# Gate and value of the last two blocks in seven half products, over named PSUM banks, with the last quarters in another order

## The chip, the core and the metric

The kernel runs on one core of a Trainium2 chip. The core has a matrix engine (TensorE, in the profile PE for matmuls and PEld for the loads of their stationary operand), VectorE (DVE), ScalarE (ACT), GpSimd (POOL) and SyncE (SP, which here only issues DMAs). They run side by side, each through its own instructions in order, and wait for each other by semaphores. SBUF is the working memory. PSUM is eight banks of 128 partitions by 512 fp32, into which TensorE writes; VectorE and ScalarE read and write PSUM too.

The metric is the time of one execution on the device in microseconds. The kernel before takes 343.21 us, the median of 7 runs between 342.92 and 343.62.

## What is computed

An attention without softmax and a gated feed-forward layer behind it:

```python
kv  = einsum('bhsd,bhse->bhde', k, v)            # 8 batches, 8 heads, 576 tokens, 64 wide
o   = einsum('bhsd,bhde->bhse', q, kv)
x   = o / sqrt(mean(o * o, -1) + 1e-6) * g_norm  # then 4608 tokens x 512
ffn = (gelu(x @ w_gate) * (x @ w_val)) @ w_out   # 512 -> 1536 -> 512
out = x + sigmoid(x @ w_res) * ffn
```

`x @ w_gate` and `x @ w_val` are called gate and value here, and `gelu(gate) * value` is the hidden tensor `hid`.

## The kernel before

**Blocks.** The 4608 tokens are worked in nine blocks of 512. Blocks 0 to 7 are the first 512 tokens of the eight batches; block 8 holds the remaining 64 tokens of every batch. The main loop (at the end of the kernel, `for blk in range(B + 1)`) writes the order of the work out by hand: a block is a list of `slots`, and after slot `s` come the pieces that `plans[blk][s]` holds. The engines keep the order in which the pieces are written.

**Slots of a block.** Slots 0 to 11 are `m_gval(blk, f)`, one for each of twelve strips `f` of 128 hidden columns: four matmuls of 128x512 for the gate, four for the value, a Gelu on ScalarE (L324) and a product on VectorE (L325) into `hid`. Slots 12 and 13 are `m_res` (L356), four times four matmuls for the residual gate, each followed by a Tanh on ScalarE (L365). Slots 14 and 15 are the product with `w_out`. In block 0 that is a plain product (`out_by_f`). In blocks 1 to 7 (`out_by_products`) it is one step of the scheme of Strassen and Winograd: both operands are cut into 2x2 quarters, and seven products of quarters (12 matmuls of 128x256 each, L431), with sums of quarters before and after them, take the place of eight. The sums of the `hid` quarters are `s_begin` (after slot 8) and `s_rest` (after slot 11), three chained VectorE operations of 128x1536 (L404); those of `w_out` were made in blocks 0 and 1. The products run on TensorE in the order A, D, A, E, A, F, A: `wA` holds running sums, `wE` starts as a copy of `wA` by ScalarE (L456), `wd` is a copy of `wD` (L458), `wF` is the sum of `wA` and `wd` by VectorE (L404). A finished quarter is multiplied with the sigmoid by VectorE (`pf`, L466) and gets `x` added by GpSimd (`fin`, L470), and SyncE stores it. Between `pf((0, 0))` and the sum `c22` stands a hook, `rest`, for pieces of other work; only block 1 uses it.

**Attention beside it.** The attention of batch b runs in the slots of block b - 1: raw loads on the GpSimd queue (`load_behind`), kv product, o product, squares and sums (L222, L224), the norm (`a_norm`, many small VectorE operations after slot 7), `a_t` (L282) and `a_x` (L296) after slots 9 to 11, and a DMA transpose into `xT` on the SyncE queue (L313, after slot 12). For b = 2, 3, 5 and 7 the remaining tokens of two batches get their `a_t` and `a_x` after slot 15 of block b - 1. So blocks 7 and 8 have no attention beside them.

**The last block.** `out_last` is the same seven products for block 8, with `wA` split in two halves, a fourth `m_res` in the middle of the products, and stores from two queues (SyncE and ScalarE, L533).

**The opening.** Batch 0 is worked by a list of words, `opening`, that interleaves loads, casts, transposes, the attention of head pairs 0 to 3 and the first eight matmul groups. `o1` and `o0` (L734) write two PSUM tiles of the pool `pmoe`; `t0` (L759, VectorE) is the last reader of the tile of `o0`; the words `g1` and `v1` (L785) start two gate tiles and two value tiles, of strips 0 and 1, for head pair 1.

**PSUM.** Two pools of four banks, `pmoe` for the feed-forward layer and `pattn` for attention. A tile that is asked for gets a bank of its pool that has come free, in the order of the program as written. The first writer of a tile waits until every reader of the former tile in its bank is done.

Of the kernel before, what the change touches and what calls it, by code (L numbers as in the profile page):

```python
# [8 lines left out]
FP32 = mybir.dt.float32  # L9
FP16 = mybir.dt.float16  # L10
# [8 lines left out]
def kernel(  # L19
# [33 lines left out]
    attnp = ctx.enter_context(tc.tile_pool(name="attnp", bufs=2))  # L53
    xp = ctx.enter_context(tc.tile_pool(name="xp", bufs=3))
    hidp = ctx.enter_context(tc.tile_pool(name="hidp", bufs=1))
    moep = ctx.enter_context(tc.tile_pool(name="moep", bufs=3))
    finp = ctx.enter_context(tc.tile_pool(name="finp", bufs=2))

    pmoe = ctx.enter_context(tc.tile_pool(name="pmoe", bufs=4, space=bass.MemoryType.PSUM))
    pattn = ctx.enter_context(tc.tile_pool(name="pattn", bufs=4, space=bass.MemoryType.PSUM))  # L60

    ctx.enter_context(tc.manual_schedule())
    nc.scalar.preload_act_table_set("sqrt_and_others")
# [78 lines left out]
    def new_block(blk):  # L142
        pool, kw = (xp, {}) if blk < B else (consts, {})
        t_t[blk] = pool.tile([P, NJ, C], FP16, tag="t" if blk < B else "tl", name="t")
        xT_t[blk] = pool.tile([P, NJ, NP, P], FP16, tag="xT" if blk < B else "xTl", name="xT")

    def attn_begin(b):
        st[b] = {
# [201 lines left out]
        m_mm(vps, wv_c, f, blk, 0, NJ)  # L350
        m_act(blk, f, gps, vps)

    def m_res(blk, j, pool=pmoe, tag="mm"):
        rps = pool.tile([P, C], FP32, tag=tag, name="rps")
        for cc in range(NP):
            nc.tensor.matmul(  # L356
                rps,
                lhsT=xT_t[blk][:, j, cc, :],
                rhs=wr16[:, cc, :],
                start=(cc == 0),  # L360
                stop=(cc == NP - 1),
            )

        th = th_all[:, j, :]
        nc.scalar.activation(out=th, in_=rps, func=AF.Tanh, scale=0.5)  # L365
        return th
# [70 lines left out]
                    skip_group_check=True,  # L437
                )

    def out_by_products(blk, later, rest=()):  # L440
        w = {}
        s_ = hid_sums

        def res(jj):
            for j in (2 * jj, 2 * jj + 1):
                m_res(blk, j)
            if jj == 1:

                pmoe.tile([P, C], FP32, tag="mm", name="none")

        def first_two():
            for n in ("D", "E", "F", "A"):
                w[n] = pmoe.tile([P, 2, CH], FP32, tag="mm", name="w" + n)
            w["d"] = finp.tile([P, 2, CH], FP32, tag="wd", bufs=1, name="wd")
            prod(w["A"], a_of(blk, 1, 1), b_of(1, 1), True)
            nc.scalar.copy(out=w["E"], in_=w["A"])  # L456
            prod(w["D"], s_[0], wo_t[:, 0], True)
            nc.scalar.copy(out=w["d"], in_=w["D"])  # L458
            for j in range(NJ):
                m_sigmoid(j)  # L460
# [48 lines left out]
            at(blk + 1, 10, lambda: fin((1, 1)), lambda: store(1))  # L509
        return [lambda: res(0), lambda: res(1), first_two, others]  # L510

    def out_last(blk):

        s_ = hid_sums

        def bank(n, pool, tag):
            return pool.tile([P, n, CH], FP32, tag=tag, name="w")

        def part(j, n, ch):
            return slice(None), slice(j, j + n), slice(ch * CH, (ch + 1) * CH)  # L520

        def gated(j, n, ch, src):
            of = part(j, n, ch)
            nc.vector.tensor_tensor(out=res_all[of], in0=th_all[of], in1=src, op=ALU.mult)  # L524

        def plus(j, n, ch, eng):
            of = part(j, n, ch)
            eng.tensor_tensor(out=res_all[of], in0=res_all[of], in1=t_t[blk][of], op=ALU.add)  # L528

        def store(j, n, c0, c1):  # L530
            for e, queue in enumerate((nc.sync, nc.scalar)):
                dst = out.rearrange("(j e s) c -> e s j c", e=2, s=S)[e, M0:S, j : j + n, c0:c1]
                queue.dma_start(out=dst, in_=res_all[e * R : (e + 1) * R, j : j + n, c0:c1])  # L533

        def run():
            wa = [bank(1, pattn, "at") for _ in range(2)]
            wd, we, wf = [bank(2, pmoe, "mm") for _ in range(3)]
            d = finp.tile([P, 2, CH], FP32, tag="wd", bufs=1, name="wd")
            for e in range(2):
                prod(wa[e], a_of(blk, 1, 1), b_of(1, 1), True, (e,))  # L540
                nc.scalar.copy(out=we[:, e : e + 1, :], in_=wa[e])
            prod(wd, s_[0], wo_t[:, 0], True)
            nc.scalar.copy(out=d, in_=wd)
            for j in range(NJ - 1):
                m_sigmoid(j)
            for e in range(2):
                prod(wa[e], s_[1], wo_t[:, 1], False, (e,))
                sub(nc.vector, wf[:, e : e + 1, :], wa[e], d[:, e : e + 1, :], ALU.add)
            prod(we, a_of(blk, 1, 2), b_of(2, 1), False)
            gated(0, 2, 0, we)  # L550
            plus(0, 2, 0, nc.gpsimd)
            m_res(blk, 3)
            m_sigmoid(3)
            prod(wf, s_[3], b_of(2, 2), False)
            gated(0, 2, 1, wf)
            plus(0, 2, 1, nc.gpsimd)
            store(0, 2, 0, C)
            for e in range(2):
                prod(wa[e], s_[2], wo_t[:, 2], False, (e,))
                sub(nc.vector, res_all[part(2 + e, 1, 1)], wa[e], d[:, e : e + 1, :], ALU.add)  # L560
            gated(2, 2, 1, res_all[part(2, 2, 1)])
            plus(2, 2, 1, nc.gpsimd)
            store(2, 2, CH, C)
            for e in range(2):
                prod(wa[e], a_of(blk, 2, 2), wo_t[:, 3], False, (e,))
                gated(2 + e, 1, 0, wa[e])
            plus(2, 1, 0, nc.gpsimd)
            plus(3, 1, 0, nc.vector)
            store(2, 2, 0, CH)

        return [lambda: [m_res(blk, j) for j in range(3)], run]

    def out_by_f(blk):

        ths, fpss, pfs = [], [], []
        slots = [lambda j=j: ths.append(m_res(blk, j)) for j in range(NJ)]

        def step(f):
            if f == 0:
                fpss.extend(pmoe.tile([P, C], FP32, tag="mm", name="fps") for _ in range(NJ))  # L580
            for j in range(NJ):
                m_ffn(blk, j, f, fpss[j])
            if NFH <= f < NFH + NJ:
# [153 lines left out]


    def f_sq(pr, j0, j1):
        first["sq", pr, j0] = sq = attnp.tile([P, j1 - j0, 2, D], FP32, tag=f"sq{j1 - j0}", name="sq")  # L740
        ps = first["o", pr].rearrange("p j (h d) -> p j h d", h=2)
        nc.scalar.activation(out=sq, in_=ps[:, j0:j1], func=AF.Square)

# [155 lines left out]
    def plan_attn(b):  # L899
# [36 lines left out]
        if rem:  # L936
            at(m, NF + 3, lambda: a_x(b, NJ), lambda: d_xT(b, NJ, NJ + 1))

    late = []
    for blk in range(B + 1):  # L940
        plan = plans[blk]
# [8 lines left out]
            plan[5] = [lambda j=j: a_x(0, j) for j in range(NJ)]  # L950
        else:
            slots = [lambda f=f: m_gval(blk, f) for f in range(NF)]
            if blk == 1:
                slots[0] = lambda: m_gval(1, 0, pattn, "at")
                plan.setdefault(3, []).append(lambda: (wo_sums(1), wo_sums(3)))
            outs = []
            slots += [lambda i=i: outs[i]() for i in range(4 if blk < B else 2)]
            plan.setdefault(NFH + 2, []).insert(0, lambda: s_begin(blk))
            def products(blk=blk, outs=outs):
                s_rest(blk)  # L960
                outs.extend(out_by_products(blk, blk == 1, amid_out.get(blk, ())) if blk < B else out_last(blk))

            plan.setdefault(NF - 1, []).append(products)
            for j, fs in enumerate(late):
# [55 lines left out]
```

## Time and profile before

| what | value |
|---|---|
| median of 7 runs | 343.21 us (342.92 to 343.62) |
| the execution that was profiled | 343.19 us |
| its span, first to last instruction | 341.4 us |
| granted clock of TensorE, mean | 0.996 |
| busy: TensorE matmuls / weight loads | 331.0 us (97%) / 186.8 us |
| busy: VectorE, ScalarE, GpSimd | 231.5, 150.1, 102.3 us |
| block 7: first gate matmul, first `m_res`, first matmul of block 8 | 267.81, 288.53, 301.15 us |
| block 8: first `m_res`, first product, last product's start | 321.87, 324.46, 333.27 us |

Times of single instructions are counted from the start of the span. 1.79 us of the profiled execution lie outside its span. A matmul's row gives its issue and a modelled end, so matmuls in a row overlap in the records; the distance of their starts is what one costs.

### The profile page before, as it was taken

The page shows a single profiled execution, that of the slowest core. Times are in us where ns is not written, and L with a number is a line of the kernel's source. Part 1 is how long each engine was busy: PE and PEld are TensorE (multiplying, and loading weights), DVE is VectorE, ACT ScalarE, POOL GpSimd, SP SyncE. Part 2 cuts the span into 40 slices and gives each one's busy share as a digit, 9 for nine tenths or more (in the row PEclk, how much of TensorE's full clock was granted, in tenths as well). Part 3 has the DMA queues.
Part 4 walks back from the last instruction along what each step waited for, and adds up shares of the span by engine and source line. Part 5 has one row for each costly group of instructions (what it writes and reads, how often), then busy time and mean ns, then how long its engine had stood idle before and what let it go on. Part 6 is the DMA issues. An engine that isn't in the chain of part 4 may idle for free.

```text
span 341.4 us, 6156 instructions
## 1 busy us (share of the span) xinstructions
PE 331.0 (97%) x2432; PEld 186.8 (55%) x2432; DVE 231.5 (68%) x439; ACT 150.1 (44%) x265; POOL 102.3 (30%) x121
## 2 busy tenths in 40 slices
PE   8899999999999999999999999999999999999992
PEld 3544454446744485448444854485447644854481
DVE  6755369489859976797479776975787745453643
ACT  3663464364354433544354525352636233523450
POOL 2782334960055029001900182004000600050013
PEclk9999999999999999999999999999999999999998
DMA  8999999599699156916591539563003210030004
GB/s 243 317 201 200 195 203 168 138 155 94 140 145 170 40 118 154 187 9 139 144 181 10 123 127 175 47 126 139 2 0 61 83 57 2 1 122 3 0 2 123
DMA packets 76399, 38.81 MB, mean 114 GB/s; under 512 B 42066, under 2 KB 73810, under 8 KB 76370
## 3 DMA queue, kind: packets, MB, share of 16 engines
q0 software_dynamic: 38752, 17.17, 40.2%
q1 hardware_dynamic: 37184, 20.71, 21.9%
q10 hardware_dynamic: 434, 0.52, 0.5%
q8 instruction: 19, 0.31, 0.4%
q14 instruction: 10, 0.08, 0.1%
HBM read 38.80 MB, written 9.44 MB: 141 GB/s over the span
## 4 chain that ended last, share of the span: by engine, by line
PE 90%; DVE 4%; DMA 3%; issue 1%; POOL 1%; POOLq 0%; SPq 0%; DVEq 0%
PE gps L336 27%; PE vps L336 26%; PE wA L431 10%; PE rps L356 8%; PE fps L373 3%; PE wD L431 3%; PE wF L431 3%; PE wE L431 3%; PE w L431 2%; PE kvp L187 2%; DMA hid_s<-in_v_dram 1%; DMA kf<-in_k_dram 1%; PE op L205 1%; DVE t L282 1%; DVE t L759 1%
## 5 line engine op out<-in xcount | busy, mean ns | idle before, releaser
L324 ACT ACTIVATE ge<-gps 128x512 f16<-128x512 f32 x108 | 64.3, 597 | 131.9 <-PE gps L336 126.6
L325 DVE TENSOR_TENSOR hid<-ge,vps 128x512 f16<-128x512 f16 x108 | 73.7, 684 | 63.6 <-PE vps L336 59.4
L336 PE MATMUL vps<-xT,wv 128*128 128x512 f16 x424 | 108.8, 379 | 0.4 <-DVE hid L325 0.4
L336 PE MATMUL gps<-xT,wg 128*128 128x512 f16 x424 | 109.0, 379 | 0.0
L470 POOL TENSOR_TENSOR osb<-osb,t 128x512 f32<-128x512 f32 x28 | 36.1, 1310 | 154.4 <-DVE osb L466 148.6
L336 PEld LDWEIGHTS <-wv 128*128 128x128 f16 x424 | 41.5, 98 | 50.6 <-issue 0.7
L336 PEld LDWEIGHTS <-wg 128*128 128x128 f16 x424 | 40.2, 98 | 45.4 <-issue 0.4
L431 PEld LDWEIGHTS <-hid_s 128*128 128x128 f16 x384 | 37.5, 98 | 5.1 <-DVE hid_s L404 0.4
L356 PE MATMUL rps<-wr,xT 128*128 128x512 f16 x144 | 32.7, 379 | 0.0
L431 PEld LDWEIGHTS <-hid 128*128 128x128 f16 x288 | 28.2, 98 | 5.1
L365 ACT ACTIVATE th<-rps 128x512 f32<-128x512 f32 x36 | 21.5, 598 | 19.0 <-PE rps L356 19.0
L356 PEld LDWEIGHTS <-xT 128*128 128x128 f16 x144 | 14.1, 98 | 16.8
L224 DVE TENSOR_REDUCE ss<-sq 128x8 f32<-128x512 f32 x32 | 20.6, 679 | 2.9 <-ACT sq L222 2.7
L431 PE MATMUL wA<-wo_ts,hid_s 128*128 128x256 f16 x168 | 20.6, 273 | 0.0
L370 ACT ACTIVATE th<-th 128x512 f32<-128x512 f32 x36 | 19.9, 622 | 0.0
L282 DVE TENSOR_TENSOR t<-op,ny 128x512 f16<-128x512 f32 x28 | 17.8, 680 | 0.1
L222 ACT ACTIVATE sq<-op 128x512 f32<-128x512 f32 x28 | 15.3, 596 | 4.5 <-PE op L205 4.1
L296 DVE TENSOR_TENSOR t<-t,g 128x512 f16<-128x512 f16 x36 | 16.2, 496 | 0.1
L404 DVE TENSOR_TENSOR hid_s<-hid 128x1536 f16<-128x1536 f16 x16 | 15.3, 954 | 0.3
L528 POOL TENSOR_TENSOR osb<-osb,t 128x512 f32<-128x512 f32 (+1 forms) x4 | 4.3, 1079 | 27.8 <-DVE osb L524 27.8
L373 PE MATMUL fps<-wo,hid 128*128 128x512 f16 x48 | 11.2, 379 | 0.0
L431 PE MATMUL wD<-wo_ts,hid_s 128*128 128x256 f16 x84 | 10.3, 273 | 0.1
(132 smaller groups left out, 316.5 us busy)
## 6 DMA issues: line engine op xcount, KB each, us to landing
out_dram<-osb SPq DMA_DIRECT2D x14, 512.0 KB, 2.7
qraw<-in_q_dram POOLq DMA_DIRECT2D x7, 512.0 KB, 8.0
k<-in_k_dram POOLq DMA_DIRECT2D x7, 512.0 KB, 9.7
v<-in_v_dram POOLq DMA_DIRECT2D x7, 512.0 KB, 11.9
out_dram<-osb SPq DMA_DIRECT2D x5, 256.0 KB, 2.8
wg<-in_moe_w_gate_dram POOLq DMA_DIRECT2D x2, 512.0 KB, 8.2
wv<-in_moe_w_val_dram POOLq DMA_DIRECT2D x2, 512.0 KB, 8.9
wo<-in_moe_w_out_dram POOLq DMA_DIRECT2D x2, 512.0 KB, 13.7
```

What stands on the lines that cost most here:

```text
L224: nc.vector.tensor_reduce(out=out_, in_=sq, op=ALU.add, axis=mybir.AxisListType.X)
L282: nc.vector.tensor_tensor(out=t, in0=o, in1=scale, op=ALU.mult)
L296: nc.vector.tensor_tensor(out=t_t[blk][:, jj, :], in0=t_t[blk][:, jj, :], in1=g16, op=ALU.mult)
L324: nc.scalar.activation(out=ge, in_=gps, func=AF.Gelu)
L325: nc.vector.tensor_tensor(out=hids[blk][:, f, :], in0=ge, in1=vps, op=ALU.mult)
L336: nc.tensor.matmul(ps[:, j0 * P : j1 * P], lhsT=w[:, cc, :], rhs=xT_t[blk][:, j0:j1, cc, :], start=(cc == 0 and j0 == 0), stop=(cc == NP - ...
L356: nc.tensor.matmul(rps, lhsT=xT_t[blk][:, j, cc, :], rhs=wr16[:, cc, :], start=(cc == 0), stop=(cc == NP - 1),)
L365: nc.scalar.activation(out=th, in_=rps, func=AF.Tanh, scale=0.5)
L370: nc.scalar.activation(out=th, in_=th, func=AF.Copy, scale=0.5, bias=0.5)
L373: nc.tensor.matmul(fps, lhsT=hids[blk][:, f, j * P : (j + 1) * P], rhs=wo16[:, f, :], start=(f == 0), stop=(f == NF - 1))
L431: nc.tensor.matmul(ps[:, e - es[0], :], lhsT=a[:, f, e * P : (e + 1) * P], rhs=b[:, f, :], start=(start and e == es[0] and f == 0), stop=( ...
L470: nc.gpsimd.tensor_tensor(out=res_all[of], in0=res_all[of], in1=t_t[blk][of], op=ALU.add)
```

## The change

**Named banks.** A class `Banks` takes the place of the two pools' choice: a tile gets the next bank of a fixed turn, or the bank that its caller names. `pmoe` owns banks 0 to 3 (the first three tiles 0, 1, 2, then the turn 3, 2, 1, 0 over and over), `pattn` banks 4 to 7. `banks_behind()` names the banks of the residual tiles and of A, D, E, F behind twelve strips; A gets the bank of the last strip's value tile.

**Seven half products.** In blocks 7 and 8 the slots 0 to 11 become three calls of `gv_group`, each for four strips (512 hidden columns). Gate and value of a group are each the product of x (512 tokens by 512) with a 512x512 piece of weights, cut into 2x2 quarters: seven products of four matmuls of 128x256 (the word `1g` is product 1 of the gate) for what eight would be. ScalarE copies A into E and the D product out of F (`E`, `d`), VectorE makes F and the fourth quarter c from A and d (`F`, `c`), ScalarE takes the Gelu of each quarter (`g11` and so on), VectorE three products into `hid` and GpSimd the fourth (`h22`, from SBUF alone). Gate and value have four banks each.

**Sums for it.** Weight sums (24 of 128x512 in fp16; the eight of group 0 as two instructions of 128x256 each) are made by VectorE after slots 0, 1, 2, 5 and 6 of blocks 3 to 6, into four new tiles and two buffers of `q16`. Token sums (four of 128x512 for each of blocks 7 and 8) are made by VectorE in the hook `rest` of blocks 6 and 7.

**The last block.** All four `m_res` stand ahead of the products; the sigmoids run in the order 2, 3, 0, 1; GpSimd prepares `u = th * d + t` for the quarter (rows 2 and 3, second half), which VectorE then finishes with two products and one sum of 128x512; VectorE adds x to the last quarter row by row; the first store is split in two.

**Small ones.** The pool of the Gelu outputs has 5 buffers for 3, `xT` has 2 for 3, the squares of the opening share one tag.

```diff
-    pmoe = ctx.enter_context(tc.tile_pool(name="pmoe", bufs=4, space=bass.MemoryType.PSUM))
-    pattn = ctx.enter_context(tc.tile_pool(name="pattn", bufs=4, space=bass.MemoryType.PSUM))
+    psum = ctx.enter_context(tc.tile_pool(name="psum", bufs=1, space=bass.MemoryType.PSUM))
+    class Banks:
+        def __init__(self, *turn, opening=()):
+            self.turn, self.opening = list(turn), list(opening)
+        def tile(self, shape, dtype, name, tag=None, bank=None):
+            if bank is None and self.opening:
+                bank = self.opening.pop(0)
+            elif bank is None:
+                bank = self.turn.pop(0)
+                self.turn.append(bank)
+            return psum.tile(shape, dtype, tag=f"bank{bank}", name=name)
+    pmoe, pattn = Banks(3, 2, 1, 0, opening=(0, 1, 2)), Banks(4, 5, 6, 7)
+    def banks_behind():
+        g0, v0, g1, v1 = pmoe.turn
+        pmoe.turn = [g1, v0, g0, v1]
+        return {0: g0, 1: g1, 2: v0, 3: g0, "A": v1, "D": g1, "E": v0, "F": g0}
...
         def run():
...
-            for j in range(NJ - 1):
+            for j in (2, 3, 0, 1):
                 m_sigmoid(j)
...
+            sub(nc.gpsimd, u, th_all[part(2, 2, 1)], d, ALU.mult)
+            sub(nc.gpsimd, u, u, t_t[blk][part(2, 2, 1)], ALU.add)
             prod(we, a_of(blk, 1, 2), b_of(2, 1), False)
             gated(0, 2, 0, we)
             plus(0, 2, 0, nc.gpsimd)
-            m_res(blk, 3)
-            m_sigmoid(3)
+            store(0, 2, 0, CH)
             prod(wf, s_[3], b_of(2, 2), False)
             gated(0, 2, 1, wf)
             plus(0, 2, 1, nc.gpsimd)
-            store(0, 2, 0, C)
+            store(0, 2, CH, C)
             for e in range(2):
                 prod(wa[e], s_[2], wo_t[:, 2], False, (e,))
-                sub(nc.vector, res_all[part(2 + e, 1, 1)], wa[e], d[:, e : e + 1, :], ALU.add)
-            gated(2, 2, 1, res_all[part(2, 2, 1)])
-            plus(2, 2, 1, nc.gpsimd)
+                gated(2 + e, 1, 1, wa[e])
+            of = part(2, 2, 1)
+            sub(nc.vector, res_all[of], res_all[of], u, ALU.add)
             store(2, 2, CH, C)
             for e in range(2):
                 prod(wa[e], a_of(blk, 2, 2), wo_t[:, 3], False, (e,))
                 gated(2 + e, 1, 0, wa[e])
-            plus(2, 1, 0, nc.gpsimd)
-            plus(3, 1, 0, nc.vector)
+                plus(2 + e, 1, 0, nc.vector)
             store(2, 2, 0, CH)
...
+    def token_sums(blk, eng):
...
+        return [
+            lambda: one(0, (0, 1), (0, 0)),
+            lambda: one(1, (1, 1), 0),
+            lambda: one(2, (1, 1), (0, 1)),
+            lambda: one(3, (1, 0), 1),
+        ]
+    def gv_group(blk, g, banks, amid=()):
...
+        for word in """1g 1v Eg 5g Ev 5v dg 6g dv 6v Fg 2g Fv 2v 7g g11 7v cg 3g cv 3v h11 g22 4g g12 h12 * 4v g21 h22 h21""".split():
...
+    units = [(n, g) for g in range(NF // GF) for n in "gv"]
+    all_sums = [f for u in units for f in weight_sums(u, nc.vector)]
+    sums_in = {3: all_sums[0:5], 4: all_sums[5:10], 5: all_sums[10:16], 6: all_sums[16:24]}
+    SUM_SLOTS = (0, 0, 1, 2, 2, 5, 5, 6)
...
+            sevens = blk in LAST
+            if sevens:
+                slots = [None] * NF
+                ends = banks_of(blk)
+                mid = [lambda: s_begin(blk)]
+                for g in range(NF // GF):
+                    slots[GF * g] = lambda g=g: gv_group(blk, g, ends[g], mid if g == 2 else ())
...
+            if blk + 1 in LAST:
+                amid_out.setdefault(blk, []).extend(token_sums(blk + 1, nc.vector))
```

In `one(i, x, y)` a number names an earlier sum of the same four: the second token sum reads the first, and the fourth the second. In `gv_group` the word list gives the order in which the pieces are written: a digit first is a product on TensorE, `E` and `d` are ScalarE's copies, `F` and `c` VectorE's sums, `g11` to `g22` the Gelus, `h11` to `h22` the products into `hid`, and `*` in the third group is `s_begin`.

## The prediction

> **What bounds the kernel.** I read the page's first and fourth part, then the chain of waits from 118 us on.
>
> ```profile
> PE 331.0 (97%) x2432; PEld 186.8 (55%) x2432; DVE 231.5 (68%) x439; ACT 150.1 (44%) x265; POOL 102.3 (30%) x121
> PE 90%; DVE 4%; DMA 3%; issue 1%; POOL 1%; POOLq 0%; SPq 0%; DVEq 0%
> ```
>
> TensorE is the bound: from 21 us to the last product it has one hole in the records (0.44 at 113.8), so a matmul saved there is time saved, and any wait put ahead of a matmul is time lost. The chain gives prices by issue:
>
> ```profile
> 288.69 3.45 PE rps L356 x16
> 292.15 1.31 PE wA L431 x12
> ```
>
> A 128x512 matmul costs 3.45 / 16 = 0.2158 us, a 128x256 one 1.31 / 12 = 0.1092.
>
> **What the half products take away.** A block's gate and value are 96 matmuls of 128x512, 20.72 us (block 7: 267.81 to 288.53). After, 3 x 2 x 7 x 4 = 168 of 128x256: 18.35. That is 2.37 less per block, **-4.75 us** for two, if nothing waits.
>
> **Do the groups keep pace?** A product takes 0.437. A consumer starts 0.20 after its product's last issue (block 6: twelve from 258.64 end issuing at 259.95, ScalarE starts at 260.15). Counted from a group's start: products 1g, 1v, 5g, 5v end at 0.44, 0.87, 1.31, 1.75; ScalarE's four copies (0.57 to 0.59 each, L456, L458) end at 1.23, 1.78, 2.35, 2.90; VectorE's F sums (0.70, L404; a next one can start after 0.60) run 2.40 to 3.10 and 3.00 to 3.70. 7g is due at 3.49, 7v at 3.93: 0.18 to spare. Sums c end at 4.85 and 5.45; 4v is due at 5.68: again 0.18. ScalarE is busy 4.7 and VectorE 4.8 of 6.11 us. So a steady group costs nothing, narrowly; every bank that it takes over had its last reader earlier. Below zero is excluded: TensorE can't go faster than issue.
>
> **The opening.** The turn is 3, 2, 1, 0 behind 0, 1, 2. `idle` has bank 0, `o1` 1, `o0` 2; so the gate tiles of `g1` get 3 and 2, and the second must wait for the last reader of `o0`, `t0`. Today it is the second *value* tile that gets that bank:
>
> ```profile
> 16.34 0.59 PE L785 MATMUL gps<-xT,wg 128*128 128x512 f16 x2 [0.24 <-ACT xT L776]
> 16.77 0.39 PE L769 MATMUL xtp<-ident,t 128*128 128x128 f16 x4
> 17.01 0.39 PE L785 MATMUL vps<-xT,wv 128*128 128x512 f16 x1
> 17.99 0.38 PE L785 MATMUL vps<-xT,wv 128*128 128x512 f16 x1 [0.59 <-DVE t L759]
> ```
>
> The wait for `t` is there now, but behind the transposes of pair 2. After, they stand behind it: they go from 16.77 to 18.20, and ScalarE's copy of them from 17.19 to 18.62. On ScalarE the root of pair 3 (17.78) is queued behind that copy, on VectorE the reciprocal and both halves of `t3` (18.41 to 19.17) behind the root: now until 20.6. `g0`, at 19.52 today behind the transposes of `t3`, comes at 20.77. From there both run at matmul pace: **+1.25 us**. Bounds: 0, were the bank free earlier, and 1.43, the whole shift.
>
> The hole in TensorE grows from 0.59 to 1.43. The granted clock stayed at 1.00 from 15.20 to 18.60 us, where TensorE was busy 2.56 of 3.40 us; I cost it at nothing. The Trainium skill ("TensorE: Matmul & The Clock Gate", "A second HAM failure mode: psum-queue depth-cycling") speaks against this change here: many short idles between groups of matmuls can bring the clock to half. By that page's window of 3.4 us one such fall would add an estimated 1.7 us to the sum.
>
> **Bank A.** The first product of a block's output now takes the bank of strip 11's value, so it waits for the last `hid`; today it has a residual's bank. In block 2:
>
> ```profile
> 117.98 0.68 DVE L325 TENSOR_TENSOR hid<-ge,vps 128x512 f16<-128x512 f16 x1
> 118.10 1.47 PE L431 MATMUL wA<-wo,hid 128*128 128x256 f16 x12
> 119.71 1.48 PE L431 MATMUL wD<-wo_ts,hid_s 128*128 128x256 f16 x12
> ```
>
> `wA` moves to 118.71 and `wD` to 120.02: +0.31 (strip 10's value also waits longer, which this swallows). Blocks 4 and 6 have `hid` ending within 0.01 of `wA`'s start: +0.06 each. **+0.43 us**; bounds 0 and 0.8.
>
> **Weight sums.** An fp16 sum of 128x512 has the nearest row in L296, 0.415 us. They hide in VectorE's holes ahead of the strips: in block 6 it waits 1.04, 1.04, 1.47, 1.40 us for TensorE ahead of strips 0 to 3 and 0.39, 1.04 ahead of 6 and 7, for eight sums of 3.3 us together; the last has its end at 248.1, strip 7 is ready at 248.55. **0**; bound above 0.4 per block, one sum late, 1.6.
>
> **Token sums.** These have no such hole. VectorE in the output of block 6, from the timeline:
>
> ```profile
> 264.25 0.69 DVE L466 TENSOR_TENSOR osb<-th,wE 128x512 f32<-128x512 f32 x1 [0.71 <-ACT th L370]
> 265.45 0.69 DVE L404 TENSOR_TENSOR osb<-wA,wd 128x512 f32<-128x512 f32 x1 [0.51 <-PE wA L431]
> 268.69 0.87 DVE L282 TENSOR_TENSOR t<-o,ny 128x512 f16<-128x512 f32 x1
> 269.59 1.26 DVE L296 TENSOR_TENSOR t<-t,g 128x512 f16<-128x512 f16 x1
> ```
>
> GpSimd in the same timeline, its second add there:
>
> ```profile
> 268.97 1.60 POOL L470 TENSOR_TENSOR osb<-osb,t 128x512 f32<-128x512 f32 x1
> ```
>
> The operation of L296 in the whole run (shortest, median, longest in ns):
>
> ```profile
> L296 DVE TENSOR_TENSOR t<-t,g x36: 409/415/1266, 29.0 to 269.6; 128x512 f16<-128x512 f16 x36
> ```
>
> The four sums stand between the first two lines, and the last A product (issue at 266.50) must wait until the second, `c22`, has read `wA`. Alone: sums at 264.85, 265.31 (it reads the first), 265.64, 265.98; `c22` 266.30 to 267.00; A at 267.05, +0.55. But GpSimd starts its add at 265.01, right in them, and the L296 line shows what that does: beside an add the same operation took 1.26, ending 0.28 after the add ended (270.57). The add in turn stood still while `t` (268.69) ran, took its turn between `t` and L296, which reads `t`, and lasted 1.60 for 1.16. So: first sum to 265.27, the add to 266.28, second sum to 266.56, `c22` 267.15 to 267.84, A at 267.89: +1.39. I take this, the nearest row being the same operation: **+2.78 us** for blocks 6 and 7; bounds 1.1 and 3.3 (the add goes first). The Trainium skill ("SBUF — State Buffer", "Who interferes with whom") calls such a meeting a lock that whoever issues first holds for its whole instruction. By that page the sum is +2.78 and the upper bound falls away, for the first sum issues before the add; the rows alone leave it open.
>
> **Block 7's first group.** At its start VectorE still has `pf`, `t` and L296 of the remaining tokens. Today its next operation starts at 270.78, 2.97 after the block's start; Fg is due at 2.40 and 7g at 3.49 needs it 0.70 later, so 7v waits: +0.39. With the block's end later, the adds fall ahead of `t` as well as of L296; Fg starts at 3.5, 7g at 4.25 for 3.49, 7v 0.16 later still: **+0.92**. I take the second, which goes on from the step before; bounds 0.2 and 1.3. Block 8 has only `pf` in front, done at 0.95: 0.
>
> **The tail.** Counted from the first product of block 8, the last is issued at 9.17 before and after (the fourth `m_res` only moves). Today the last sum ends 2.07 behind that (336.65 against 334.58), and the end of the span comes 4.75 later with the store. After, GpSimd has u (two of 1.15, from the sigmoid at 4.55 on), then the two adds, until 9.24; VectorE's sum with u reads two SBUF tiles at 8.5, so it waits for the second add and ends at 9.8; then product, add, product, add of 0.43 each with gaps: 11.4, that is 2.23 behind: **+0.16**. Without the meeting it is 1.68: -0.39; bounds -0.4 and +0.5. Three early stores of 0.6 us issue lie ahead of it.
>
> **Sum.** -4.75 + 1.25 + 0.43 + 0 + 2.78 + 0.92 + 0.16 = +0.79. The profiled execution took 343.19, 0.02 below the median: **344.0 us**.
>
> **Rivals.**
> *The meeting doesn't bite* (the other side, not slower): the four sums run through ahead of the add. Place: after `pf((0, 0))` of blocks 6 and 7. Tokens 1.1, first group 0.2, tail -0.39: -4.75 + 1.25 + 0.43 + 1.1 + 0.2 - 0.39 = -2.16, 341.0. For it: the first sum issues before the add. Against: three L296 at 1.26. It ends faster as soon as the two stalls are under 0.65 each with the rest as forecast. Chance 0.24.
> *The opening isn't touched*: `t0` moves ahead or the bank is free: 344.0 - 1.25 = 342.7. Against: the wait on `t` stands in the rows. 0.08.
> *The groups don't keep pace*: three steps in a chain (copy, copy, F) each 0.1 later use up the 0.18 twice per group; 0.24 x 6 = +1.5: 345.4. For it: no row has this chain. 0.16.
> *The halves cost more than 0.1092*: the moving operand comes in two runs of 128. Against: today's runs are 128 long and issue at pace. At 0.1233 the gain is gone: 348.7. 0.02.
>
> **Chances.** The forecast has 0.50, its own range 343.0 to 345.1, 0.18 of it under 343.9. What 7 runs can tell from no change is 0.2%, 0.69 us. Faster: 0.24 and a little of the second rival, 0.26. Same: 0.18 and most of the second rival, 0.25. Slower: 0.32 + 0.16 + 0.02, 0.49. The range reaches from the first rival to the third: 341.0 to 345.5.
>
> **What would show it.** Block 7's 168 matmuls of gate and value in 19.3 us and block 8's in 18.35; a TensorE wait on `t` L759 at `gps`; on `osb` L404 ahead of the last `wA` of blocks 6 and 7, 1.3 to 1.4 each, with a token sum of over 1.1 us; on F at block 7's start. No such waits and a start of block 8 more than 4 us early: the first rival. Waits on F and c in all six groups: the third.

## The result and the profile after

The changed kernel takes 343.7 us (median of 27 runs) where the kernel before takes 343.39 (64 runs): a ratio of 1.0003, 95% interval 0.9992 to 1.0014. The difference can't be told from none. Medians are over all runs, while ratios leave out the few in which a kernel took some per cent longer at a lower granted clock, so a ratio is not the quotient of two medians. The profiled execution took 344.5 us, with a span of 342.6 and a granted clock of 0.995.

The same two parts of the page as before, busy time and the chain:

```profile
PE 327.5 (96%) x2576; PEld 200.8 (59%) x2576; DVE 257.6 (75%) x498; ACT 161.2 (47%) x289; POOL 110.2 (32%) x127
PE 86%; DVE 6%; DMA 3%; ACT 2%; issue 1%; POOL 0%; SPq 0%; DVEq 0%
```

TensorE has 3.5 us less to do, and the span is not shorter. VectorE has 26 us more, and its share of the chain went from 4 to 6%. So the place to look is TensorE's waits (what waited, for whom, total us, times, longest). These four are the ones that bear on the change:

```profile
PE wA L452 <- DVE osb L425: 2.3, 2, 1.2
PE gps L957 <- DVE t L931: 1.3, 1, 1.3
PE Ag L682 <- DVE Fg L703: 0.8, 1, 0.8
PE vps L357 <- DVE hid L346: 0.8, 1, 0.8
```

The first three were not there before; `vps` on `hid` was, with 0.4, and a `vps` waited 0.6 for `t`. The list also has `idle` with 1.2, as before, and two waits of `kvp` on `v` ahead of block 0, 0.8 and 0.7 where they were 0.6 and 0.2. For each of the first three I read the timeline.

**The opening**, TensorE. The second gate tile of `g1` waits where a value tile waited before, and the transposes (L941) stand behind it:

```profile
17.21 0.38 PE L957 MATMUL gps<-xT,wg 128*128 128x512 f16 x1 [0.24 <-POOL wg L984]
18.88 0.38 PE L957 MATMUL gps<-xT,wg 128*128 128x512 f16 x1 [1.29 <-DVE t L931]
19.09 0.38 PE L941 MATMUL xtp<-ident,t 128*128 128x128 f16 x4
```

**The output of block 6**, VectorE, GpSimd and the last A product. L488 is GpSimd's addition of x, the four `ts` are the token sums:

```profile
267.55 0.42 DVE L425 TENSOR_TENSOR ts<-xT 128x512 f16<-128x512 f16 x1
267.71 1.27 POOL L488 TENSOR_TENSOR osb<-osb,t 128x512 f32<-128x512 f32 x1 [29.07 <-DVE osb L484]
268.00 1.26 DVE L425 TENSOR_TENSOR ts<-xT,ts 128x512 f16<-128x512 f16 x1
269.19 0.41 DVE L425 TENSOR_TENSOR ts<-xT 128x512 f16<-128x512 f16 x1
269.52 0.41 DVE L425 TENSOR_TENSOR ts<-xT,ts 128x512 f16<-128x512 f16 x1
269.86 0.68 DVE L425 TENSOR_TENSOR osb<-wA,wd 128x512 f32<-128x512 f32 x1
270.59 1.47 PE L452 MATMUL wA<-wo_ts,hid 128*128 128x256 f16 x12 [1.23 <-DVE osb L425]
```

The second sum needs 0.42 us and takes 1.26. It ends at 269.26, 0.28 behind the end of GpSimd's addition (268.98). `c22`, the line with `osb<-wA,wd`, stands behind all four sums and starts late by their time and by the 0.84 us that the second takes too long. The A product, which must wait until `c22` has read `wA`, waits 1.23.

**The start of block 7**, GpSimd, VectorE and the product 7g:

```profile
271.21 4.22 POOL L488 TENSOR_TENSOR osb<-osb,t 128x512 f32<-128x512 f32 x3 [2.23 <-DVE osb L484]
272.77 1.64 DVE L303 TENSOR_TENSOR t<-o,ny 128x512 f16<-128x512 f32 x1
274.44 1.27 DVE L317 TENSOR_TENSOR t<-t,g 128x512 f16<-128x512 f16 x1
275.63 0.68 DVE L703 TENSOR_TENSOR Fg<-Ag,d 128x512 f32<-128x512 f32 x1
276.37 0.60 PE L682 MATMUL Ag<-ts,ws 128*128 128x256 f16 x4 [0.82 <-DVE Fg L703]
```

The two steps of the remaining tokens take 2.9 us beside GpSimd's three additions, where they took 0.87 and 1.26 in the kernel before, and Fg comes 3.74 us after the block's start (271.89).

A table of stages puts these into one sum. A stage is the distance of two starts of issue: "gv" from a block's first gate matmul to its first `m_res`, "out" from there to the next block's first gate matmul. Tail: from the last product's end of issue to the last sum. Store: from there to the end of the span. Stages that are not named differ by 0.01 at most.

| stage (us) | before | after | difference |
|---|---|---|---|
| start of block 0 | 16.34 | 17.21 | +0.87 |
| gv 0 | 22.18 | 23.46 | +1.28 |
| out 1 | 12.81 | 12.92 | +0.11 |
| gv 2 and out 2 | 36.23 | 36.55 | +0.32 |
| gv 3 to gv 6 (weight sums) | 89.74 | 89.74 | 0 |
| out 4 | 12.62 | 12.68 | +0.06 |
| out 6 | 12.62 | 14.07 | +1.45 |
| gv 7 | 20.72 | 19.48 | -1.24 |
| out 7 | 12.62 | 13.90 | +1.28 |
| gv 8 | 20.72 | 18.34 | -2.38 |
| out 8 | 12.70 | 12.64 | -0.06 |
| tail | 2.08 | 2.21 | +0.13 |
| store | 4.75 | 4.12 | -0.63 |

Without the first line the differences add to +0.32, and the medians differ by +0.31. I don't count the first line to the change: the program up to there does the same work in all fourteen profiles of this study, and block 0 starts anywhere between 16.04 and 17.86 in the thirteen of the changed kernel and its variants, which has the 16.34 of the kernel before inside. Nor "out 1": it is 12.80 or 12.81 in all thirteen others.

So the half products give what their count says, and five new delays, less a shorter store, leave nothing of it.

### The profile page after: what moved, and what is told of

It is laid out like the page before. It is cut to its first block, busy times and chain, and to the rows that moved or that the text cites. A ratio compares the mean times of both kernels' runs of the same rounds, so it can differ in the third digit from the quotient of the medians.

```text
span 342.6 us, 6525 instructions
## 1 busy us (share of the span) xinstructions
PE 327.5 (96%) x2576; PEld 200.8 (59%) x2576; DVE 257.6 (75%) x498; ACT 161.2 (47%) x289; POOL 110.2 (32%) x127
## 4 chain that ended last, share of the span: by engine, by line
PE 86%; DVE 6%; DMA 3%; ACT 2%; issue 1%; POOL 0%; SPq 0%; DVEq 0%
PE gps L357 21%; PE vps L357 20%; PE wA L452 9%; PE rps L377 8%; PE Av L682 3%; PE Ag L682 3%; PE fps L394 3%; PE wD L452 3%; PE w L452 2%; PE wF L452 2%; PE wE L452 2%; DMA kf<-in_k_dram 2%; PE kvp L208 2%; PE Fv L682 2%; PE Fg L682 2%; DMA hid_s<-in_v_dram 2%
## 5 line engine op out<-in xcount | busy, mean ns | idle before, releaser
L345 ACT ACTIVATE ge<-gps 128x512 f16<-128x512 f32 x84 | 50.1, 597 | 98.6 <-PE gps L357 97.8
L357 PE MATMUL vps<-xT,wv 128*128 128x512 f16 x328 | 84.2, 379 | 0.8 <-DVE hid L346 0.8
L357 PE MATMUL gps<-xT,wg 128*128 128x512 f16 x328 | 84.4, 380 | 0.0
L346 DVE TENSOR_TENSOR hid<-ge,vps 128x512 f16<-128x512 f16 x84 | 57.2, 682 | 32.8 <-PE vps L357 28.9
L488 POOL TENSOR_TENSOR osb<-osb,t 128x512 f32<-128x512 f32 x28 | 36.2, 1312 | 138.9 <-DVE osb L484 133.1
L357 PEld LDWEIGHTS <-wv 128*128 128x128 f16 x328 | 32.1, 98 | 39.6 <-issue 1.1
L357 PEld LDWEIGHTS <-wg 128*128 128x128 f16 x328 | 30.7, 98 | 34.7 <-DMA xT<-t 0.2
L682 PEld LDWEIGHTS <-ws 128*128 128x128 f16 x192 | 18.8, 98 | 3.3 <-issue 1.2
L719 POOL TENSOR_TENSOR hid<-ge,c 128x512 f16<-128x512 f16 x6 | 7.0, 1166 | 25.6 <-ACT ge L713 25.6
L452 PE MATMUL wA<-wo_ts,hid 128*128 128x256 f16 x84 | 10.3, 272 | 2.3 <-DVE osb L425 2.3
```

The lines of the kernel that those rows point to most:

```text
L345: nc.scalar.activation(out=ge, in_=gps, func=AF.Gelu)
L346: nc.vector.tensor_tensor(out=hids[blk][:, f, :], in0=ge, in1=vps, op=ALU.mult)
L357: nc.tensor.matmul(ps[:, j0 * P : j1 * P], lhsT=w[:, cc, :], rhs=xT_t[blk][:, j0:j1, cc, :], start=(cc == 0 and j0 == 0), stop=(cc == NP - ...
L452: nc.tensor.matmul(ps[:, e - es[0], :], lhsT=a[:, f, e * P : (e + 1) * P], rhs=b[:, f, :], start=(start and e == es[0] and f == 0), stop=( ...
L488: nc.gpsimd.tensor_tensor(out=res_all[of], in0=res_all[of], in1=t_t[blk][of], op=ALU.add)
L682: nc.tensor.matmul(out_[:, r, :], lhsT=lhsT, rhs=rhs, start=(first and r == 0 and c == 0), stop=(c == 1), skip_group_check=True,)
```

## The experiments

My theory: each delay is a separate stage with the cause named in the prediction (bank of the opening, bank A, the meeting of VectorE and GpSimd over the token sums, the remaining tokens in front of Fg). Rivals: VectorE's work is too much wherever GpSimd stands; or what one repair frees is waited for elsewhere. Unless said, an edit is to the changed kernel alone.

### The opening's banks

```diff
-    pmoe, pattn = Banks(3, 2, 1, 0, opening=(0, 1, 2)), Banks(4, 5, 6, 7)
+    pmoe, pattn = Banks(3, 2, 1, 0, opening=(1, 2, 0)), Banks(4, 5, 6, 7)
```

> The changed kernel with the first three named banks as 1, 2, 0 in place of 0, 1, 2, so that strip 1's value tile, not its gate tile, gets the bank of o0. Theory (the opening pays for the bank order): the wait of 1.3 us of a gate tile on t goes, 0.6 of it comes back at the value tile, g0 comes 1.25 to 1.28 earlier, and the time falls by that from the changed kernel's, to about 342.3. Rival (the opening is paced by its loads and casts, the wait lies in their shadow): within 0.3 us of the changed kernel, 343.5.

Measured: 342.6 us (9 runs), ratio to the kernel before 0.9982 (0.9972 to 0.9992). The timeline of this kernel, TensorE:

```profile
16.82 0.59 PE L957 MATMUL gps<-xT,wg 128*128 128x512 f16 x2 [0.24 <-ACT xT L948]
17.25 0.39 PE L941 MATMUL xtp<-ident,t 128*128 128x128 f16 x4
18.48 0.38 PE L957 MATMUL vps<-xT,wv 128*128 128x512 f16 x1 [0.63 <-DVE t L931]
```

Both gate tiles run at once, the transposes follow, and the value tile waits 0.63 as it did before. gv 0 is 22.19 for 23.46, a gain of 1.27; the median is 1.1 lower. The theory holds.

### The token sums ahead of the quarter

```diff
             prod(w["E"], a_of(blk, 1, 2), b_of(2, 1), False)
+            ahead = blk + 1 in LAST
+            for f in rest if ahead else ():
+                f()
             pf((0, 0), w["E"])
-            for f in rest:
+            for f in () if ahead else rest:
                 f()
```

> The changed kernel with the four token sums of blocks 6 and 7 ahead of pf((0, 0)) in place of behind it, so before GpSimd's add begins and in a hole of 0.7 us. Theory (the sums meet GpSimd's add, and the last A product waits for c22): the waits of 1.23 and 1.12 us of wA on osb go, no token sum is over 0.5 us, and the time falls by 2.6 to 3.3, to about 340.7. Rival (VectorE has no room there, 1.4 us of sums cost that wherever they stand): c22 is as late as before or the A product ahead of it waits for F, and the time falls by less than 1.

Measured: 340.25 us (4 runs), ratio 0.9908 (0.9895 to 0.9921). Block 6's output in the timeline:

```profile
265.49 0.42 DVE L425 TENSOR_TENSOR ts<-xT 128x512 f16<-128x512 f16 x1
265.94 0.42 DVE L425 TENSOR_TENSOR ts<-xT,ts 128x512 f16<-128x512 f16 x1
266.28 0.42 DVE L425 TENSOR_TENSOR ts<-xT 128x512 f16<-128x512 f16 x1
266.61 0.42 DVE L425 TENSOR_TENSOR ts<-xT,ts 128x512 f16<-128x512 f16 x1
...
267.55 0.69 DVE L425 TENSOR_TENSOR osb<-wA,wd 128x512 f32<-128x512 f32 x1
267.71 1.15 POOL L488 TENSOR_TENSOR osb<-osb,t 128x512 f32<-128x512 f32 x1 [29.74 <-DVE osb L484]
268.54 1.47 PE L452 MATMUL wA<-wo_ts,hid 128*128 128x256 f16 x12
```

The sums take up the 0.71 us in which VectorE waited for the sigmoid and delay the quarter by the rest, which holds up no product: the A product has no wait, and out 6 and out 7 are 12.68 and 12.62. There is a second thing to see: `c22` (267.55) runs beside GpSimd's addition and neither is longer than alone, 0.69 and 1.15. It reads one operand from PSUM; the sums that suffered read two from SBUF. The kernel before shows the same with GpSimd first: `c22` at 265.45, 0.44 us into the addition that starts at 265.01, took 0.69 (the row and the addition's start stand in the prediction). Block 7's gate and value gained too (18.71 for 19.48), because the remaining tokens' first step now takes 0.87 us for 1.64; that is why the time fell by 3.45 us, more than the 2.6 to 3.3 that were expected.

### GpSimd's addition behind the next one

```diff
-            if not later:
-                fin((0, 0))
...
+            fin((0, 0))
```

The second line stands behind `fin((0, 1))`; the token sums stay where the change has them.

> The token sums stay where the change has them, and only GpSimd's first addition of a block's end is moved, behind the one that follows it, so that it no longer runs beside the token sums. Theory (the meeting): without GpSimd beside them the four sums take about 0.42 us each instead of 0.42, 1.26, 0.41 and 0.41, so the last A product of blocks 6 and 7 waits some 0.84 us less each: 14.07 and 13.90 us fall to about 13.2 and 13.05 in the two stages, and the time by 1.5 us (1.2 to 1.8), to about 342.1. Rival (VectorE's own work is the whole cost, wherever GpSimd stands): the four sums are queued ahead of the sum that the last A product needs, and the wait stays at 1.1 to 1.2 us in each block; no change.

Measured: 341.98 us (6 runs), ratio 0.9951 (0.9933 to 0.9968). Block 6's output:

```profile
266.99 0.42 DVE L425 TENSOR_TENSOR ts<-xT 128x512 f16<-128x512 f16 x1
267.45 0.42 DVE L425 TENSOR_TENSOR ts<-xT,ts 128x512 f16<-128x512 f16 x1
...
269.19 1.47 PE L452 MATMUL wA<-wo_ts,hid 128*128 128x256 f16 x12 [0.39 <-DVE osb L425]
...
269.81 2.65 POOL L488 TENSOR_TENSOR osb<-osb,t 128x512 f32<-128x512 f32 x2 [30.44 <-DVE osb L484]
```

With GpSimd away the same sums in the same place cost 0.84 us less per block (13.23 and 13.06). So of 1.39 us in block 6 0.84 are the meeting, and 0.55 are four sums that stand in front of `c22`. The prediction's figures for the sums alone (+0.55) and beside the addition (+1.39) are both in the rows.

### The sums apart from each other

In every row so far GpSimd got in where a VectorE operation reads the output of the one before it. I thought that this was the condition.

```diff
-            for f in rest:
+            spread = blk + 1 in LAST
+            for f in [rest[0], rest[2], rest[1]] if spread else rest:
                 f()
...
             sub(nc.vector, c22, w["A"], w["d"], ALU.add)
+            if spread:
+                rest[3]()
```

> The changed kernel with the token sums of blocks 6 and 7 in the order 0, 2, 1, and sum 3 behind c22, so that no token sum reads the one directly before it; GpSimd's addition stays where it is. In every row so far GpSimd got in between two VectorE operations of which the second reads the first's output. Theory (it gets in only there): the three sums run through at 0.42 us each ahead of the addition, c22 starts 1.24 us earlier, and the output stages of blocks 6 and 7 fall from 14.07 and 13.90 us to about 12.85 and 12.65: the time falls by 2.4 us, to about 341.3. Rival (GpSimd gets in behind whatever instruction it meets): the second sum still takes about 1.26 us and only the sum that was moved is saved, 0.34 us per block: 13.73 and 13.56, the time 0.7 us lower, about 343.0.

Measured: 342.18 us (12 runs), ratio 0.9963 (0.9934 to 0.9991). The theory fell, the rival's stages came: 13.73 and 13.56.

```profile
266.65 1.71 DVE L425 TENSOR_TENSOR ts<-xT 128x512 f16<-128x512 f16 x2
266.81 1.27 POOL L488 TENSOR_TENSOR osb<-osb,t 128x512 f32<-128x512 f32 x1 [29.07 <-DVE osb L484]
268.29 0.41 DVE L425 TENSOR_TENSOR ts<-xT,ts 128x512 f16<-128x512 f16 x1
```

The first row holds two sums of which neither reads the other; they take 1.71 us and end 0.28 behind GpSimd's addition. In the experiment with the sums ahead two such sums took 0.75 (266.28 to 267.03). The addition, issued during the first, holds up the second all the same. The time fell by more than the rival's 0.7, because block 7's gate and value also fell to 18.71, as with the sums ahead.

### Bank A

```diff
-        pmoe.turn = [g1, v0, g0, v1]
-        return {0: g0, 1: g1, 2: v0, 3: g0, "A": v1, "D": g1, "E": v0, "F": g0}
+        pmoe.turn = [v0, v1, g0, g1]
+        return {0: g0, 1: g1, 2: v0, 3: g0, "A": g1, "D": v0, "E": v1, "F": g0}
```

> The changed kernel with other banks behind the twelve strips: A in that of residual 1, D residual 2, E strip 11's value, F residual 3. Theory (wA waits for the last hid in block 2, a little in blocks 4 and 6): 0.43 + 0.06 us less, about 343.1. Rival (block 2 waits for VectorE's sums anyway, so that the bank only moves the wait): no change, 343.6.

Measured: 343.27 us (12 runs), ratio 1.0002 (0.9989 to 1.0016). By time this can't be told from the changed kernel, so the time decides nothing between theory and rival. In the stages the gain is there: out 2 is 12.67 for 12.97, out 4 12.62 for 12.68, out 6 14.01 for 14.07, together 0.42 us.

### The remaining tokens later

```diff
-            at(m, NF + 3, lambda: a_t(b, NJ))
+            at(*((m, NF + 3) if b < B - 1 else (b, 4)), lambda: a_t(b, NJ))
...
-            at(m, NF + 3, lambda: a_x(b, NJ), lambda: d_xT(b, NJ, NJ + 1))
+            at(*((m, NF + 3) if b < B - 1 else (b, 4)), lambda: a_x(b, NJ), lambda: d_xT(b, NJ, NJ + 1))
```

> The changed kernel with the remaining tokens' a_t, a_x and transpose of batch 7 behind block 7's second group in place of behind block 6. Theory (they stand in front of block 7's first F sum on VectorE, stretched by GpSimd's adds): the wait of 0.82 us of 7g on F and the 0.16 of 7v go, 1.0 to 1.15 us less, about 342.5. Rival (the first group is late because ScalarE's copies and the first F sum are slow in a new stage): block 7's gate and value still take over 19 us, no change.

Measured: 343.89 us (11 runs), ratio 1.0016 (1.0005 to 1.0026): no gain, the expectation failed. gv 7 is 19.57. The wait for Fg is gone, but the timeline of group 0 shows another:

```profile
277.25 0.63 ACT L713 ACTIVATE ge<-c 128x512 f16<-128x512 f32 x1 [0.94 <-DVE c L703]
277.91 0.69 DVE L703 TENSOR_TENSOR c<-Av,d 128x512 f32<-128x512 f32 x1 [0.69 <-ACT ge L713]
278.65 0.60 PE L682 MATMUL Av<-ts,wv 128*128 128x256 f16 x4 [0.42 <-DVE c L703]
```

VectorE waited 0.69 us for a Gelu before it wrote the value's c, although c doesn't need that Gelu's result. The Gelu is the reader of the gate's c. Both c tiles take buffers of the tag `o32`, of which there are two, and the remaining tokens' attention output, now waiting for its moved step, holds one of them. That was an argument; the next run tests it.

### The same with a third buffer

```diff
-        st[b]["o"][NJ] = o32 = attnp.tile([P, C], FP32, tag="o32", name="o32")
+        st[b]["o"][NJ] = o32 = attnp.tile([P, C], FP32, tag="o32", bufs=3, name="o32")
...
-                dst = sb["c", u] = attnp.tile([P, 2, PR], FP32, tag="o32", name="c")
+                dst = sb["c", u] = attnp.tile([P, 2, PR], FP32, tag="o32", bufs=3, name="c")
```

> Like e5_rest_later, with a third buffer for the kind of tile that holds the remaining tokens' attention output and the copies c. Theory (the buffer): in e5_rest_later the waiting tile held one of two buffers until its moved step, so the value's c had to wait until ScalarE had read the gate's c, by 0.42 and 0.49 us in groups 0 and 1. With a third buffer both waits go, and block 7's gate and value takes 18.3 to 18.5 us where the changed kernel takes 19.48 and e5_rest_later 19.57; the time falls by 1.0 to 1.15 us against the changed kernel, to about 342.6. Rival (VectorE is simply full in those groups): the waits of the value's fourth product on c stay, and the stage stays near 19.5.

Measured: 342.53 us (10 runs), ratio 0.9969 (0.9958 to 0.998). gv 7 is 18.34, the same as gv 8: no wait is left in block 7's groups. The two c sums of group 0 are now 0.61 us apart, where they were 1.39:

```profile
275.19 0.69 DVE L703 TENSOR_TENSOR c<-Ag,d 128x512 f32<-128x512 f32 x1 [0.38 <-PE Ag L682]
275.80 0.68 DVE L703 TENSOR_TENSOR c<-Av,d 128x512 f32<-128x512 f32 x1
```

### The four repairs together

The edits of the banks of the opening, of the sums ahead, of bank A and of the remaining tokens with the third buffer, and no other.

> All four repairs together: opening banks 1, 2, 0; bank A as in e4_bank_a; token sums ahead as in e2_sums_ahead; the remaining tokens' steps later with the third buffer. If each term is a stage of its own, as the table of stages says, they add: -1.28 (opening), -0.44 (bank A over three blocks), -1.39 and -1.28 (token sums), -1.14 (block 7's first group), together -5.5 us, to about 338.2 us (337.6 to 338.8), a ratio of about 0.985 to the kernel before. Rival (what one repair frees is waited for elsewhere): block 7's gate and value stays above 18.6, or the sums ahead delay the sums of the last A product once bank A is free earlier; the sum then falls short by 0.4 us or more.

Measured: 338.18 us (5 runs), ratio 0.984 (0.9821 to 0.986). Against the changed kernel's 343.7 that is -5.5, as the stages add. What TensorE waits for longest in this kernel:

```profile
PE idle L845 <- DVE zeros L818: 1.2, 1, 1.2
PE vps L357 <- DVE hid L346: 0.8, 1, 0.8
PE vps L960 <- DVE t L934: 0.6, 1, 0.6
```

The rows on `osb`, on Fg and of `gps` on `t` are gone. gv 7 and gv 8 are 18.34, out 6 and out 7 12.62, as in the kernel before. The halves' whole gain stands, and nothing moved to another place.

### The tail without the meeting

```diff
             gated(0, 2, 1, wf)
-            plus(0, 2, 1, nc.gpsimd)
             store(0, 2, CH, C)
```

> The changed kernel without GpSimd's second addition of x at the end (the output of the first two token strips lacks x in the second half of its columns). Theory (the meeting at the end): VectorE's sum with u, 1.23 us beside GpSimd's addition, takes about 0.68 us alone, and the last sum ends about 1.65 us behind the last product instead of 2.21. Rival (it is the size of the operands that makes the sum long): it stays at 1.2, and the tail at 2.2. One look: read in the tail's rows, not in the time.

This kernel leaves out x in the second half of the columns of the first two strips of the output, so only its rows are read, not its time. One execution, 343.3 us. First the changed kernel, then this one, VectorE's sum with u in the timeline:

```profile
334.07 2.27 POOL L546 TENSOR_TENSOR osb<-osb,t 128x512 f32<-128x512 f32 x2
...
335.65 1.23 DVE L425 TENSOR_TENSOR osb<-osb,u 128x512 f32<-128x512 f32 x1
```

```profile
333.46 1.16 POOL L546 TENSOR_TENSOR osb<-osb,t 128x512 f32<-128x512 f32 x1
...
335.04 0.69 DVE L425 TENSOR_TENSOR osb<-osb,u 128x512 f32<-128x512 f32 x1
```

1.23 became 0.69, and the tail is 1.67 for 2.21. The 0.54 us by which the sum got shorter are the whole gain of the tail.

### One store for the first strips

```diff
             plus(0, 2, 0, nc.gpsimd)
-            store(0, 2, 0, CH)
...
             plus(0, 2, 1, nc.gpsimd)
-            store(0, 2, CH, C)
+            store(0, 2, 0, C)
```

> The changed kernel with the first two strips stored in one piece behind their second sum, as the kernel before stores them, instead of in two halves. Question: the stretch from the last sum to the end of the span is 4.12 us in the changed kernel and 4.75 in the kernel before. Theory (halved stores): the first half left early and no longer shares the queues with the last stores; with one piece the stretch is back at 4.5 us or more. Rival (spacing: the last two stores are issued 1.44 us apart in the changed kernel, 0.81 before): it stays at 4.0 to 4.2. One look, read from the trace's rows, not from the time.

One execution, 345.5 us. The stretch from the last sum to the end is 5.11 us for 4.12. The DMA issues of the last stretch (queue, count, size, median us from issue to landing), first the changed kernel, then this one:

```profile
out_dram<-osb SPq DMA_DIRECT2D x4, 128.0 KB, 2.7
out_dram<-osb ACTq DMA_DIRECT2D x4, 128.0 KB, 3.0
```

```profile
out_dram<-osb SPq DMA_DIRECT2D x1, 256.0 KB, 3.3
out_dram<-osb ACTq DMA_DIRECT2D x1, 256.0 KB, 4.6
out_dram<-osb SPq DMA_DIRECT2D x2, 128.0 KB, 3.5
out_dram<-osb ACTq DMA_DIRECT2D x2, 128.0 KB, 4.2
```

By these medians the 128 KB stores take 0.8 to 1.2 us longer to land when a large one stands ahead of them. One execution is enough here, for the stretch hardly varies: in the nine profiles that have the changed kernel's tail as it is, it lies between 4.02 and 4.21. So the split first store is what makes the end shorter in the changed kernel; the last two stores are issued 1.4 and 1.3 us apart, so their spacing isn't it. The split does two things that this run can't tell apart: the pieces are half as large, and the first of them is issued at 335.25, where the whole is issued at 336.36. Why the stretch is longer than the 4.75 of the kernel before, which stored in one piece too, stays open.

### Another order in the tail

```diff
             of = part(2, 2, 1)
-            sub(nc.vector, res_all[of], res_all[of], u, ALU.add)
-            store(2, 2, CH, C)
             for e in range(2):
                 prod(wa[e], a_of(blk, 2, 2), wo_t[:, 3], False, (e,))
                 gated(2 + e, 1, 0, wa[e])
-                plus(2 + e, 1, 0, nc.vector)
+                if e == 0:
+                    sub(nc.vector, res_all[of], res_all[of], u, ALU.add)
+                    store(2, 2, CH, C)
+            plus(2, 2, 0, nc.vector)
             store(2, 2, 0, CH)
```

> The changed kernel with VectorE's sum with u between the two last gated products, and the two last additions of x in one instruction. Tail: the sum with u starts when GpSimd's addition is nearly done (336.3 on the changed kernel's clock), so it takes 0.7 instead of 1.23 us, and the last sum ends about 1.75 us behind the last product instead of 2.21. Stores: the last two are then issued about 1.05 us apart instead of 1.44; if the spacing sets the last stretch (rival of e10_one_store) it grows from 4.12 towards 4.5, and the time gains nothing; if not, it stays at 4.0 to 4.2 and the gain is 0.45 us, which is read from the rows.

One execution, 343.46 us. The tail is 1.68, the store's stretch 4.38: half of the gain of 0.53 is given back. The last stores are closer together here, which suggests that the spacing counts too, for less than the split; 4.38 is only a little outside the 4.02 to 4.21 of the unchanged tail, and no run changes the spacing alone.

The same edit on top of the four repairs:

> The four repairs of e8_all and the order of e11_tail_order. If the tail gains 0.45 us and the last store's stretch stays, 337.75 us (337.4 to 338.2), a ratio of 0.983 to the kernel before; if the stores take back what the tail gains, 338.2 as e8_all.

Measured: 337.88 us (5 runs), ratio 0.9847 (0.9833 to 0.986). Tail 1.69, store 4.28: 0.31 us less than with the four repairs alone (2.20 and 4.08), and the medians differ by 0.30, but they were taken beside different runs of the kernel before and the intervals of the ratios overlap. This has the lowest median; by the ratios it can't be told from the four repairs alone. Both are faster than the kernel before and than the changed kernel.

## Why the prediction came out as it did

Step by step, predicted and measured by the stages:

- **Half products**: -2.37 per block; block 8 gave -2.38, and block 7 the same once its wait was taken away. The halves issue at the pace of 0.1092, and the groups keep pace: no wait on F or c stands in block 8. The third and fourth rivals are out.
- **The opening**: +1.25; +1.28, and moving the banks takes it away. The cause is shown. The clock didn't fall: the windows from 16 to 18 and from 18 to 20 us have a granted clock of 1.00 with TensorE busy 1.34 and 1.12 of 2.00 us. The fall to half that the prediction weighed (the Trainium skill, "TensorE: Matmul & The Clock Gate", "A second HAM failure mode: psum-queue depth-cycling": frequent short idles between groups of matmuls make the clock swing to half and back) does not show in these rows.
- **Bank A**: +0.43; +0.32 in block 2 and 0.06 in block 4, and 0.06 of block 6's. Shown in the stages, too small for the times.
- **Weight sums**: 0; gv 3 to gv 6 are equal to 0.01.
- **Token sums**: +1.39 in each block; 1.39 and 1.28. The first rival, that the meeting doesn't bite, is out: the second sum took 1.26 and ended 0.28 behind the add, to the hundredth as the L296 row of the kernel before did. The experiments split the cost into 0.84 of meeting and 0.55 of work. The Trainium skill ("SBUF — State Buffer", "Who interferes with whom") says that a VectorE instruction with two SBUF inputs contends with a GpSimd instruction that reads SBUF, and one with at most one SBUF input, outside the two-port modes, doesn't. The rows agree: 1.26 for 0.42 with two from SBUF, 0.69 for 0.69 with one from PSUM.
- **Block 7's first group**: +0.92; +1.14 (2.38 - 1.24). The mechanism was right. Fg was forecast 3.5 us behind the block's start and came at 3.74, as the first of the two steps was lengthened to 1.64 us from 0.87; the stage lost 0.22 more.
- **The tail**: +0.16; +0.13, by the meeting that was named.
- **The store**: the step that failed. The prediction put it as "the end of the span comes 4.75 later with the store" and carried that figure over, and of the split first store it counted only the time to issue. It is 4.12 after, -0.63. With one store it is 5.11, so the split is worth 0.99, which the prediction left out. The other 0.36, by which the changed kernel with one store is longer than the kernel before, is not explained. With this term the sum would have been +0.16 and the time 343.4.

So the forecast of +0.79 was right in its mechanisms and missed 0.63 at the end, which moves the case from a little slower to no difference (+0.32 by stages, +0.31 by medians). The measured 343.7 us lies within the forecast's own range of 343.0 to 345.1, in the part under 343.9 to which it gave a chance of 0.18; "slower", its likeliest outcome, did not come. Misses of both signs (0.22 too little in block 7's first group, 0.11 too much in the second token sums) helped the total a little. The profiled execution lies a little over the forecast because block 0 started 0.87 later in it than in the profile of before.

## What to carry to other kernels

Fewer matmuls on a bound TensorE are worth their count times their issue, and each operation put ahead of what its next product needs takes some of it back: here 4.75 us were earned in two places and given back in five, and moving a few lines recovered them. Before adding work to VectorE, look where it waits and put the work into that wait, ahead of whatever releases GpSimd. When a step is moved later, the buffer that it reads is held longer; count the tiles of its tag that others ask for meanwhile.

## What the runs showed of the hardware

- GpSimd's addition, issued while VectorE's first sum ran, held up the second, whether or not the second reads the first (1.26 us for 0.42, and 1.71 for 0.75 of two). Both times the second ended 0.28 us behind the addition.
- In that meeting its own length hardly grew: 1.27 us for 1.15. The cost fell on VectorE's second sum.
- How long the last stores take depends on the stores ahead of them: pieces of 128 KB landed in 2.7 and 3.0 us (medians of the two queues) where all stores were of 128 KB, and in 3.5 and 4.2 behind one of 256 KB on each queue, which was also issued 1.11 us later than the first piece of 128 KB. One run shows this, and size and lateness are not told apart.
